# Selection of 32 keys and a gated second attention on one core: statistics under one number, half-row transposes, a minimum on VectorE, sums read block by block

## The chip, the cores and the metric

The kernel runs on one core of one Trainium2 chip. The metric is device time of one execution in microseconds, smaller is better; the time of before is the median of three runs.

## The reference

Eight batches of eight heads, 576 positions, head size 64. The first stage keeps in each row of scores the 32 largest, takes a softmax over them and multiplies by v. The second stage is an attention of four experts with a causal mask, on the first stage's output, gated to two experts a position.

```python
scores = scale * np.matmul(q, k.transpose(0, 1, 3, 2))
kth = np.partition(scores, -top_k, axis=-1)[..., -top_k:-top_k + 1]
scores = np.where(scores >= kth, scores, -1000000000.0)
attn = np.exp(scores - np.max(scores, axis=-1, keepdims=True))
attn = attn / (np.sum(attn, axis=-1, keepdims=True) + 1e-09)
x = np.matmul(attn, v)                      # heads joined: (8, 576, 512)
for e in range(4):                          # second stage
    q, k, v = x @ wq[e], x @ wk[e], x @ wv[e]
    a = softmax(scale * q @ k.T, causal)    # divided by its sum + 1e-9
    out += gate_e * (a @ v @ wo[e])         # gate: softmax over the best two of x @ w_gate
```

## The kernel before

The work is cut into 32 pairs of heads, four to a batch. A pair has nine tiles of 128 rows of scores (tile 8 holds the last 64 queries of both heads), handled three at a time.

For each three tiles TensorE computes scores (through the helper `mm`, L522), and ScalarE copies them to SBUF (L722, tile `s`). VectorE then narrows the 576 scores of a row to 168 candidates in tile `cand`. It takes the maximum of the two halves (f1, L737, into `fa`) and their minimum (f3, L740, into `fb`), the maximum of the halves of `fa` (f2, L743, into `fc`), and the maximum of the halves of `fc` (f4, L747, into `cand`). The minima that belong to f2 and f4 are computed on GpSimd, on the bit patterns as integers, as sum less maximum: L753 and L755 for f2, L760 and L762 (`lesser(2)`, `lesser(3)`) for f4. MAX8 and MATCH_REPLACE8 (L766 to L780) then find the 32 largest, eight at a time. The first replacement changes the maxima in `cand`, so it waits until L760 has read them.

The mask of what is left out is made on ScalarE (L839). TensorE transposes the scores and adds the mask times a large negative number (L915 for whole tiles, L929 and L522 for tile 8), ScalarE takes the exponential (L954, under one number `under` that holds for all rows), and TensorE multiplies by v (`av`). In tile 8 the halves of the rows belong to different heads: eight transposes of 64 rows are followed by two plain products with the identity, for the 64 keys at the ends.

The function `stats` makes each row's divisor from the 32 chosen scores: GpSimd subtracts the row's largest (L971) and writes that largest against `under` (L974), ScalarE takes the exponential (L977), VectorE the sum (L980), then follow a logarithm (L994), a subtraction on GpSimd (L998) and an exponential (L1001). L990 and L991 put a test value into the tile `ind`, which counts the candidates (L819, L826); a second, slow program runs after the first where the counts at the end don't come out.

When a batch's four pairs are done, `moe` projects q, k and v of the experts, computes scores turned round, takes exponentials into four tiles `ptm` (L1543), and makes their sums over the keys by a product with ones. Beforehand GpSimd adds the blocks of keys that meet the same queries (`plus`, L1563 to L1567, tile `prb`; VectorE in the last batch), so that this product reads the joint block once. The product with v (`avm`) reads every block.

The order is a table of task numbers, `ORDER`; each engine executes its tasks in that order. The table comes with the kernel, and dependencies and buffers set the waits.

Of the kernel before, what the change touches and what calls it, by code (L numbers as in the profile page):

```python
# [11 lines left out]
I32 = mybir.dt.int32  # L12
# [13 lines left out]
REACH = 1600.0  # L26
# [238 lines left out]
ADDED = (SUMMED[0], (512, ((0, None, 0, 0, 320), (4, 1, 448, 256, 64))))  # L265
# [240 lines left out]
def kernel(ctx, tc, qk, vL, wq, wk, wv, wo, out):  # L506
# [193 lines left out]
    def topk(w, general):  # L700
# [3 lines left out]
        for g in range(3):  # L704
# [123 lines left out]
            def later(due=pl.due, c=c, ind=w.ind, done=[t] if g < 2 else list(w.topped), compare=compare, count=count, g=g):  # L828
                keep, pl.due = pl.due, due
                a = add("POOL", 1050 if g < 2 else 1300, compare, done, bufs=[c, ind, w.top], prio=1)  # L830
                if g == 2:
                    pl.due += 0.3
                    counts.append(add("ACT", act(1530, False, 1, 1), count, [a, w.spread], bufs=[ind], prio=1))
# [935 lines left out]
```

## Time and profile before

| | us |
|---|---|
| median of three runs (lowest, highest) | 1074.46 (1070.68, 1081.57) |
| the profiled execution | 1079.49 |
| its span, first to last instruction | 1077.5 |
| TensorE busy in it | 1008.5 |
| VectorE busy | 986.6 |
| ScalarE busy | 862.2 |
| GpSimd busy | 805.6 |

Busy times are of one profiled execution. PE is TensorE, PEld its weight load, DVE VectorE, ACT ScalarE, POOL GpSimd, SP the engine that issues transfers. L747 is line 747 of the kernel before. An instruction's time runs from its start to its end and so holds what it waits for once it has begun. Idle time before an instruction is put down to what ended it. The granted clock of TensorE was 0.968 of full speed over the span.

### The profile page before, as it was taken

How to read it: one execution, taken by the hardware profiler on the slowest of the kernel's cores; microseconds unless marked ns; L12 is line 12 of the kernel's file. 1: busy time of each engine (PE TensorE's matmuls, PEld its weight loads, DVE VectorE, ACT ScalarE, POOL GpSimd, SP SyncE). 2: the span in 40 equal slices, each digit the busy share in tenths (PEclk: the TensorE clock that was granted, in tenths of full speed). 3: DMA queues.
4: the chain of work that ended last, by engine and by line, in shares of the span. 5: the costliest groups of instructions: out<-in, count | busy, mean ns of one | idle time of the engine just before them, and what ended most of it. 6: DMA issues, size and time to landing. Idle time of an engine off the chain costs nothing.

```text
span 1077.5 us, 26037 instructions
## 1 busy us (share of the span) xinstructions
PE 1008.5 (94%) x8819; PEld 730.9 (68%) x8819; DVE 986.6 (92%) x4271; ACT 862.2 (80%) x1512; POOL 805.6 (75%) x869
## 2 busy tenths in 40 slices
PE   7687889999999999999999999999999899999996
PEld 4454559666786668766886668766786657855794
DVE  8999898999999999899999999999999999999643
ACT  5676776988789896988789887899878887798744
POOL 4777776897779887898779877698769776698600
PEclk7798889999999999999999999999999999999999
DMA  3311211113113230232222131112203131120102
GB/s 114 101 42 49 73 43 55 45 42 98 51 38 90 63 91 1 70 91 86 56 70 72 43 104 51 55 50 68 84 28 84 42 103 47 43 59 13 59 2 80
DMA packets 66428, 66.21 MB, mean 61 GB/s; under 512 B 16183, under 2 KB 48878, under 8 KB 66286
## 3 DMA queue, kind: packets, MB, share of 16 engines
q1 hardware_dynamic: 66126, 64.24, 20.7%
q8 instruction: 71, 1.16, 0.4%
q14 instruction: 71, 0.58, 0.2%
q10 hardware_dynamic: 160, 0.22, 0.1%
HBM read 54.76 MB, written 9.66 MB: 60 GB/s over the span
## 4 chain that ended last, share of the span: by engine, by line
DVE 37%; PE 29%; POOL 16%; ACT 11%; issue 3%; DMA 2%; SPq 1%; POOLq 0%; DVEq 0%; ACTq 0%
PE slot L522 25%; DVE top L775 8%; DVE cand L780 8%; DVE fa L737 5%; PE slot L915 4%; DVE cand L766 4%; DVE fb L740 3%; ACT s L722 2%; DVE fc L743 2%; ACT mask L839 2%; ACT pt L954 2%; DVE cand L771 2%; DVE cand L747 2%; POOL fa L753 2%; DVE cand L770 2%
## 5 line engine op out<-in xcount | busy, mean ns | idle before, releaser
L775 DVE MAX8 top<-cand 128x8 f32<-128x72 f32 (+1 forms) x1152 | 243.4, 266 | 0.7
L839 ACT ACTIVATE mask<-s,top 128x576 bf16<-128x576 f32 x288 | 215.1, 771 | 30.8 <-DVE top L775 30.1
L954 ACT ACTIVATE pt<-slot,under 128x512 f32<-128x512 f32 (+3 forms) x320 | 217.9, 701 | 21.4 <-PE slot L522 19.0
L780 DVE MATCH_REPLACE8 cand<-top,cand 128x72 f32<-128x72 f32 (+1 forms) x864 | 206.5, 248 | 0.0
L522 PE MATMUL slot<-raw 64*128 64x288 f32 (+1 forms) x1280 | 197.3, 448 | 9.6 <-ACT s L722 5.2
L722 ACT ACTIVATE s<-slot 128x576 f32<-128x576 f32 x288 | 178.8, 649 | 32.9 <-PE slot L522 32.1
L915 PE MATMUL slot<-identr,s 128*128 128x128 f32 x1184 | 187.0, 288 | 10.1 <-ACT pt L954 4.8
L522 PE MATMUL slot<-pt,vt 128*64 128x320 f32 (+1 forms) x1280 | 174.2, 419 | 2.8 <-DMA vt<-in_vL_dram 1.8
L753 POOL TENSOR_TENSOR fa<-fa,fc 128x432 int32<-128x432 int32 x96 | 115.9, 1207 | 74.8 <-DVE fc L743 74.6
L915 PEld LDWEIGHTS slot<-identr,s 128*128 128x128 f32 x1184 | 133.5, 145 | 48.4 <-ACT s L722 10.9
L522 PE MATMUL slot<-negi,mask 128*128 128x128 bf16 (+3 forms) x1504 | 134.5, 221 | 19.0 <-ACT mask L839 18.6
L522 PEld LDWEIGHTS slot<-pt,vt 128*64 128x64 f32 x1280 | 90.4, 140 | 75.6 <-issue 7.5
L522 PEld LDWEIGHTS slot<-raw 64*128 64x128 f32 (+1 forms) x1280 | 95.7, 180 | 60.9 <-ACT s L722 12.8
L819 POOL TENSOR_TENSOR ind<-cand,top 128x504 bf16<-128x504 f32 x96 | 113.4, 1181 | 18.6 <-DVE top L775 10.4
L522 PEld LDWEIGHTS <-mask 128*128 128x128 bf16 (+2 forms) x1504 | 98.0, 100 | 42.8 <-ACT mask L839 24.3
L737 DVE TENSOR_TENSOR fa<-s 128x864 f32<-128x864 f32 x95 | 115.9, 1221 | 5.0 <-ACT s L722 3.2
L740 DVE TENSOR_TENSOR fb<-s 128x864 f32<-128x864 f32 x95 | 113.2, 1192 | 3.8 <-ACT s L722 3.2
L755 POOL TENSOR_TENSOR fa<-fa 128x432 int32<-128x432 int32 x96 | 113.5, 1182 | 3.6
L766 DVE MAX8 cand<-fb 128x8 f32<-128x288 f32 x288 | 112.1, 443 | 0.6
L760 POOL TENSOR_TENSOR cand<-fc,cand 128x216 int32<-128x216 int32 x96 | 68.7, 715 | 56.1 <-DVE cand L747 54.4
L762 POOL TENSOR_TENSOR cand<-cand,fc 128x216 int32<-128x216 int32 x96 | 72.4, 754 | 1.8
L780 DVE MATCH_VALUE_LOAD cand<-top,cand 128x8 f32 x864 | 66.8, 77 | 6.5 <-POOL cand L760 5.8
(161 smaller groups left out, 1803.4 us busy)
## 6 DMA issues: line engine op xcount, KB each, us to landing
raw<-in_qk_dram SPq DMA_DIRECT2D x127, 144.0 KB
vt<-in_vL_dram SPq DMA_DIRECT2D x32, 320.0 KB
raw<-in_qk_dram SPq DMA_DIRECT2D x127, 72.0 KB
rb<-turned SPq DMA_DIRECT2D x93, 64.0 KB
ot<-scale SPq DMA_DIRECT2D x32, 128.0 KB
out_dram<-prs SPq DMA_DIRECT2D x14, 256.0 KB
out_dram<-prb SPq DMA_DIRECT2D x14, 256.0 KB
rb<-turned SPq DMA_DIRECT2D x62, 32.0 KB
```

The costliest lines, as they stand in the source:

```text
L522: nc.tensor.matmul(o, l, r, start=start, stop=stop, skip_group_check=True)
L722: nc.scalar.activation(s3.t[:, n], sl.t[:, 224:224 + S], AF.Copy)
L737: v.tensor_tensor(out=fa.t, in0=s3.t[:, :, 0:288], in1=s3.t[:, :, 288:576], op=OP.max)
L740: v.tensor_tensor(out=fb.t, in0=s3.t[:, :, 0:288], in1=s3.t[:, :, 288:576], op=OP.min)
L753: nc.gpsimd.tensor_tensor(out=r, in0=r, in1=m, op=OP.subtract)
L755: nc.gpsimd.tensor_tensor(out=l, in0=l, in1=r, op=OP.add)
L766: v.max(out=c.t[:, n, 2, 48:56], in_=fb.t[:, n])
L775: v.max(out=w.top.t[0][:, j, 8 * r:8 * r + 8], in_=c.t[:, n, :, 0:24 if r < 2 else 55])
L780: v.match_replace(out=src, in_values=src, imm_value=LOW, in_to_replace=w.top.t[0][:, j, 8 * r:8 * r + 8])
L839: nc.scalar.activation(w.mask[j].t[:, n], s3.t[:, n], AF.Relu, bias=w.top.t[0][:, j, 31:32], scale=-1.0)
L915: nc.tensor.matmul(sl.t[:, d], src[:, c:c + P], identf, start=i % 4 == 0, stop=False, is_transpose=True, skip_group_check=True)
L954: nc.scalar.activation(out, src, AF.Exp, bias=under[r], scale=0.125)
```

## The change

Four parts, and the table `ORDER` written anew.

- Statistics: one exponential of the 32 chosen scores under the number `under`, their sum and its inverse on VectorE; GpSimd only writes the two test values (sum and inverse, each less 2.0e17) into `ind`, which grows from 1530 to 1539 elements.
- Tile 8: the two plain products become two more transposes of half rows. One of them covers 64 keys that belong to a neighbour as well, so ScalarE takes its exponential in two pieces.
- The minimum that belongs to f4 is one VectorE operation (f7) in place of L760 and L762.
- The product with ones reads every block of keys; the joint block and its additions go.

```diff
-REACH = 1600.0
+REACH = 2.0e17
...
-    IND = ring("ind", [P, 1530], BF, 1)
+    IND = ring("ind", [P, 1539], BF, 1)
...
-                if n == 2:
-                    nc.gpsimd.tensor_tensor(out=small, in0=r, in1=big, op=OP.subtract)
...
-                    nc.gpsimd.tensor_tensor(out=small, in0=small, in1=l, op=OP.add)
+            def f7(fc=fc, c=c):
+                l, r = [fc.t[:, :, o:o + 72].rearrange("p n (k a) -> p n k a", k=3) for o in (0, 72)]
+                v.tensor_tensor(out=c.t[:, :, :, 24:48], in0=l, in1=r, op=OP.min)
...
-            less = add("POOL", 600, lambda lesser=lesser: lesser(2), [t], bufs=[fc, c], prio=-8, tag="lessC")
+            t7 = add("DVE", 295, f7, [t2], bufs=[fc, c], prio=P0)
...
-            t7 = add("POOL", 600, lambda lesser=lesser: lesser(3), [less], bufs=[fc, c], prio=-8, tag="lessD")
...
-                    t = add("DVE", 3 * dve(n) + 165, lambda r=r, rep=rep: rep(r), [t] + ([less] if r == 0 else []),
+                    t = add("DVE", 3 * dve(n) + 165, lambda r=r, rep=rep: rep(r), [t],
...
-                ends = [(slice(64 * x, 64 * x + 64), o + 512 - 512 * x) for x in range(2)]
+                todo += [(lo, o + 512, slice(0, 64)), (hi, o - 64, slice(512, 576))]
...
-                for r, c in ends:
-                    mm(sl.t[r, 512:576], src[:, c:c + 64], identf[:, r])
...
-                    parts = [(al, 256, 0, 9, 64)]
+                    parts = [(al, 256, 0, 9, 64), (lo, 0, 4, 1, 64)]
...
+        def weights():
+            nc.scalar.activation(st.t[0], m32(), AF.Exp, bias=under, scale=0.125)
+
+        def inverse():
+            v.reciprocal(st.t[2], st.t[1][:, 0])
+
+        def spread():
+            g.tensor_scalar(w.ind.t[:, 1521:1530], st.t[1][:, 0], -REACH, None, op0=OP.add)
+            g.tensor_scalar(w.ind.t[:, 1530:1539], st.t[2], -REACH, None, op0=OP.add)
...
-        t = add("POOL", 760, s1, w.topped + ([] if w.general else made), bufs=b1, prio=0)
-        if not w.general:
-            t2 = add("POOL", 200, s2, w.topped + based, bufs=b1, prio=0)
-            t2 = w.spread = add("POOL", 300, spread, [t2], bufs=[st, w.ind], prio=0)
-        t = add("ACT", act(288, False), s3, [t], bufs=[st], prio=0)
-        t = add("DVE", dve(288), s4, [t], bufs=[st], prio=0)
...
+            t = add("ACT", act(288, False, 1), weights, w.topped + made + based, bufs=b1, prio=0)
+            t = add("DVE", dve(288), s4, [t], bufs=[st], prio=0)
+            t = add("DVE", 80, inverse, [t], bufs=[st], prio=0, tag="s5")
+            w.spread = add("POOL", 400, spread, [t], bufs=[st, w.ind], prio=0)
...
-                for k, n in ((0, 640), (1, 640), (2, 384)):
-                    pres.append(add("DVE" if final else "POOL", dve(n) if final else pool(n), lambda k=k, plus=plus: plus(k),
...
-                                   joint()[:, h] if u is None else ptm.t[u][r, h, o:o + m],
+                                   ptm.t[u][r, h, o:o + m],
...
-                a1 = add("PE", 1350, lambda sm=sm, weigh=weigh, joint=joint: weigh(sm, lambda r, j, h: ones[r], joint=joint),
-                         exps + pres[1:], bufs=[sm, ptm, pre], prio=3, tag="sums", kind="CC")
+                a1 = add("PE", 2750, lambda sm=sm, weigh=weigh: weigh(sm, lambda r, j, h: ones[r]), exps, bufs=[sm, ptm], prio=3,
+                         tag="sums", kind="CC")
...
 ORDER = [int(x) for x in """
-3 2 0 4 5 1 133 135 136 134 7 9 8 11 10 13 52 12 14 48 53 262 15 85 16 49 17 50 18 140 19 83 20 22 26 84 260 25 21 81
...
+3 2 0 5 1 4 128 7 9 8 11 10 13 47 12 14 51 48 248 15 49 16 6 52 17 129 83 50 18 19 81 84 127 79 20 22 82 24 244 25 23
```

On VectorE, the same three tiles in the middle of the program (the 48th of 96 groups): f2 (L743, L729 after), f4 (L747, L733 after), MAX8 `top` and MATCH_REPLACE `cand`. Before:

```order
L743 TENSOR_TENSOR fc_78<-fa_76 128x432
L747 TENSOR_TENSOR cand_80<-fc_78 128x9x24
L775 MAX top_0_84<-cand_79 128x8 x3
L766 MAX cand_80<-fb_77 128x8 x3
L775 MAX top_0_84<-cand_80 128x8 x3
L780 MATCH_REPLACE cand_80<-top_0_84,cand_80 128x3x24 x3
```

After:

```order
L729 TENSOR_TENSOR fc_78<-fa_76 128x432
L733 TENSOR_TENSOR cand_80<-fc_78 128x9x24
L748 MAX cand_80<-fb_77 128x8 x3
L757 MAX top_0_84<-cand_79 128x8 x3
L757 MAX top_0_84<-cand_80 128x8 x3
L762 MATCH_REPLACE cand_80<-top_0_84,cand_80 128x3x24 x3
L744 TENSOR_TENSOR cand_80<-fc_78 128x9x24
```

The minimum (L744) stands on VectorE, here behind the first replacement; nothing on GpSimd stands between f4 and that replacement.

On GpSimd, a pair's statistics about the middle of the program (`stat`, `ind`), between pieces of other work (`fa`, `cand` the minima, `ot` the experts' gates). Before:

```order
L753 TENSOR_TENSOR fa_76<-fa_76,fc_78 128x3x144
L755 TENSOR_TENSOR fa_76<-fa_76 128x3x144
L974 TENSOR_SCALAR stat_1_90<-top_0_84,under 128x9
L990 TENSOR_TENSOR stat_1_90<-stat_1_90 128x9
L991 TENSOR_SCALAR ind_81<-stat_1_90 128x9
L760 TENSOR_TENSOR cand_79<-fc_78,cand_79 128x9x24
L971 TENSOR_TENSOR stat_0_89<-top_0_84 128x288
L1603 TENSOR_TENSOR ot_130<-prs_122,ot_130 128x576
```

After:

```order
L959 TENSOR_SCALAR ind_81<-stat_1_90 128x9
L960 TENSOR_SCALAR ind_81<-stat_2_91 128x9
L1567 TENSOR_TENSOR ot_130<-prs_122,ot_130 128x576
L738 TENSOR_TENSOR fa_76<-fa_76,fc_78 128x3x144
L740 TENSOR_TENSOR fa_76<-fa_76 128x3x144
```

Of the statistics two small additions are left, and of the minima those of f2.

On TensorE, the sums of the last batch's first half. Before:

```order
L522 MATMUL slot_63<-ptm_0_126,ones 64x256 x2
L522 MATMUL slot_63<-ptm_1_127,ones 64x128 x2
L522 MATMUL slot_63<-prb_123,ones 64x320 x2
L522 MATMUL slot_63<-ptm_1_127,ones 64x64 x2
```

After:

```order
L509 MATMUL slot_65<-ptm_0_126,ones 64x256 x2
L509 MATMUL slot_65<-ptm_1_127,ones 64x128 x2
L509 MATMUL slot_65<-ptm_2_128,ones 64x320 x2
L509 MATMUL slot_65<-ptm_1_127,ones 64x320 x2
L509 MATMUL slot_65<-ptm_3_129,ones 64x320 x2
L509 MATMUL slot_65<-ptm_0_126,ones 64x192 x2
L509 MATMUL slot_65<-ptm_1_127,ones 64x64 x2
```

Four blocks in place of the joint one, the same seven that the product with v reads.

## Rows read from the trace of the kernel before

**Rows 1.** The page, part 1: busy us (share of the span) xinstructions.

```profile
PE 1008.5 (94%) x8819; PEld 730.9 (68%) x8819; DVE 986.6 (92%) x4271; ACT 862.2 (80%) x1512; POOL 805.6 (75%) x869
```

**Rows 2.** Three stretches: start:end length, busy PE, PEld, DVE, ACT, POOL (count), clock.

```profile
20.00:200.00 180.00, 149.83 (x1176) 105.42 (x1175) 169.70 (x763) 130.87 (x227) 130.13 (x141) 0.86 0.20 58
200.00:1013.00 813.00, 788.25 (x7095) 573.27 (x7090) 781.33 (x3396) 689.19 (x1215) 660.18 (x702) 1.00 0.22 62
1020.00:1066.00 46.00, 45.97 (x414) 37.87 (x412) 19.41 (x35) 24.83 (x46) 3.85 (x10) 1.00 0.07 20
```

**Rows 3.** The page, part 4: the chain of waits, shares of the span by engine.

```profile
DVE 37%; PE 29%; POOL 16%; ACT 11%; issue 3%; DMA 2%; SPq 1%; POOLq 0%; DVEq 0%; ACTq 0%
```

**Rows 4.** VectorE's groups (busy us, mean ns), then lines with ns min/median/max.

```profile
L737 DVE TENSOR_TENSOR fa<-s 128x864 f32<-128x864 f32 x95 | 115.9, 1221 | 5.0 <-ACT s L722 3.2
L740 DVE TENSOR_TENSOR fb<-s 128x864 f32<-128x864 f32 x95 | 113.2, 1192 | 3.8 <-ACT s L722 3.2
L743 DVE TENSOR_TENSOR fc<-fa 128x432 f32<-128x432 f32 x96 | 67.9, 707 | 4.5 <-POOL cand L762 2.5
L747 DVE TENSOR_TENSOR cand<-fc 128x216 f32<-128x216 f32 x96 | 55.6, 579 | 4.2 <-POOL ind L819 0.7
...
L737 DVE TENSOR_TENSOR fa<-s x95: 1029/1058/3219, 17.3 to 1003.0; 128x864 f32<-128x864 f32 x95
L743 DVE TENSOR_TENSOR fc<-fa x96: 580/609/1698, 9.9 to 1004.7; 128x432 f32<-128x432 f32 x96
L747 DVE TENSOR_TENSOR cand<-fc x96: 354/384/1577, 10.5 to 1007.9; 128x216 f32<-128x216 f32 x96
L1232 DVE RECIPROCAL g<-g x8: 158/174/189, 174.6 to 1048.4; 128x5 f32<-128x5 f32 x8
```

**Rows 5.** Timeline about 423 us: start us, us, engine and instruction.

```profile
423.29 1.05 DVE L740 TENSOR_TENSOR fb<-s 128x864 f32<-128x864 f32 x1
423.45 1.40 POOL L760 TENSOR_TENSOR cand<-fc,cand 128x216 int32<-128x216 int32 x1 [0.63 <-DVE cand L747]
```

**Rows 6.** GpSimd: three groups, then its busy time with tiles `stat` and `prb`.

```profile
L760 POOL TENSOR_TENSOR cand<-fc,cand 128x216 int32<-128x216 int32 x96 | 68.7, 715 | 56.1 <-DVE cand L747 54.4 <-DVE top L775 1.2
L762 POOL TENSOR_TENSOR cand<-cand,fc 128x216 int32<-128x216 int32 x96 | 72.4, 754 | 1.8
L991 POOL TENSOR_SCALAR ind<-stat 128x9 bf16<-128x9 f32 x32 | 10.9, 339 | 2.8
...
0.00:1077.50 1077.50, 83.82 (x160) 0.97 0.21 61
...
0.00:1077.50 1077.50, 65.89 (x42) 0.97 0.21 61
```

**Rows 7.** Waits: engine line <- released by: us in total, times, longest.

```profile
POOL fa L753 <- DVE fc L743: 74.6, 38, 9.5
...
DVE stat L980 <- ACT stat L977: 10.1, 8, 5.0
DVE cand L780 <- POOL cand L760: 5.8, 10, 2.0
```

**Rows 8.** ScalarE's group of exponentials of 64x128.

```profile
L954 ACT ACTIVATE pt<-slot,under 64x128 f32<-64x128 f32 x32 | 11.6, 362 | 0.6
```

**Rows 9.** TensorE's timeline, tile 8 of the last pair.

```profile
1015.51 0.46 PE L929 MATMUL slot<-identr,s 64*128 64x64 f32 x8
1015.90 0.34 PE L522 MATMUL slot<-identr,s 128*64 128x64 f32 x4
1016.17 0.44 PE L522 MATMUL slot<-negi,mask 64*128 64x64 bf16 x10
```

**Rows 10.** TensorE's timeline, sums and product with v of the last batch.

```profile
1051.61 0.87 PE L522 MATMUL slot<-ptm,ones 128*64 128x256 f32 x8
...
1053.21 3.07 PE L522 MATMUL slot<-ptm,v 128*64 128x256 f32 x28
1056.21 0.87 PE L522 MATMUL slot<-s,ones 128*64 128x256 f32 x8
```

More of the change, by code (lines that the diff above doesn't have):

```diff
@@ L749, in lesser @@
             def lesser(n, fa=fa, fc=fc, c=c):
[L750 to L762 removed]
+                l, r, m = [x.bitcast(I32) for x in (fa.t[:, :, 0:144], fa.t[:, :, 144:288], fc.t)]
+                if n == 0:
+                    nc.gpsimd.tensor_tensor(out=r, in0=r, in1=m, op=OP.subtract)
+                else:
+                    nc.gpsimd.tensor_tensor(out=l, in0=l, in1=r, op=OP.add)
+            def f7(fc=fc, c=c):
+                l, r = [fc.t[:, :, o:o + 72].rearrange("p n (k a) -> p n k a", k=3) for o in (0, 72)]
+                v.tensor_tensor(out=c.t[:, :, :, 24:48], in0=l, in1=r, op=OP.min)
             def f6(fb=fb, c=c):
@@ L832, in later @@
                     pl.due += 0.3
-                    counts.append(add("ACT", act(1530, False, 1, 1), count, [a, w.spread], bufs=[ind], prio=1))
+                    counts.append(add("ACT", act(1539, False, 1, 1), count, [a, w.spread], bufs=[ind], prio=1))
                 pl.due = keep
@@ L926, in turned @@
                         for i in range(4) for x in range(2)]
-                ends = [(slice(64 * x, 64 * x + 64), o + 512 - 512 * x) for x in range(2)]
+                todo += [(lo, o + 512, slice(0, 64)), (hi, o - 64, slice(512, 576))]
                 for i, (r, c, d) in enumerate(todo):
-                    nc.tensor.matmul(sl.t[:, d], src[r, c:c + P], identf[r, r], start=i < 2, stop=False, is_transpose=True,
+                    out, m = (sl.t[lo, d], 64) if i == 8 else (sl.t[:, d], P)
+                    nc.tensor.matmul(out, src[r, c:c + m], identf[r, r], start=i < 2, stop=False, is_transpose=True,
                                      skip_group_check=True)
-                for r, c in ends:
-                    mm(sl.t[r, 512:576], src[:, c:c + 64], identf[:, r])
-                for r, c, d in todo:
-                    mm(sl.t[:, d], mask[r, c:c + P], negi[r, r], stop=True)
-                for r, c in ends:
-                    mm(sl.t[r, 512:576], mask[:, c:c + 64], negi[:, r], stop=True)
+                for i, (r, c, d) in enumerate(todo):
+                    out, m = (sl.t[lo, d], 64) if i == 8 else (sl.t[:, d], P)
+                    mm(out, mask[r, c:c + m], negi[r, r], stop=True)
             def exp(sl=sl, pt=pt, j=j):
                 if j == 8:
-                    parts = [(al, 256, 0, 9, 64)]
+                    parts = [(al, 256, 0, 9, 64), (lo, 0, 4, 1, 64)]
                 elif j == 5:
@@ L954, in exp @@
                         nc.scalar.activation(out, src, AF.Exp, bias=under[r], scale=0.125)
-            need = [w.masked[j]] + ([w.masked[j - 1]] if j in (2, 4, 5, 7) else [w.masked[1]] if j == 0 and w.general else [])
+            need = [w.masked[j]] + ([w.masked[j - 1]] if j in (2, 4, 5, 7) else [w.masked[1]] if j == 0 and w.general else [w.masked[7]] if j == 8 else [])
             full = j in (0, 2, 4, 5, 7)
@@ L958, in turn @@
                     kind="TM" if j < 8 else "ZZ", tag="turned" if full else "turned8" if j == 8 else "turned4")
-            d = act(576, True, 1) if j == 8 else act(640, True, 1) + (200 if j == 5 else 0) if full else act(512, True, 1)
+            d = act(576, True, 1) + 200 if j == 8 else act(640, True, 1) + (200 if j == 5 else 0) if full else act(512, True, 1)
             w.es[j] = add("ACT", d, exp, [a] + ([] if w.general else based) + ([w.es[0]] if j == 5 else []), bufs=[sl, pt],
@@ L986, in s5 @@
             g.memset(z[:, 1], 0.0)
-        def spread():
-            z = st.t[1]
-            g.tensor_tensor(out=z[:, 2], in0=z[:, 1], in1=z[:, 1], op=OP.mult)
-            g.tensor_scalar(w.ind.t[:, 1521:1530], z[:, 2], -REACH, None, op0=OP.add)
         def s6():
```

47 lines of the change are left out of this document (12 added, 35 removed), and 394 rows, old and new, of the table ORDER.

## The prediction

> **What bounds the kernel now.** I read the busy times first. TensorE is busy 94% of the span, VectorE 92%, GpSimd 75% [rows 1]. An average over stages with different limits says little, so the busy time by stretch comes next [rows 2]. From 200 to 1013 us, where the selection of one pair, the product with v of another and the experts' work of a batch run beside each other, TensorE is busy 788.3 of 813 us and VectorE 781.3: 24.8 and 31.7 us idle. From 20 to 200 us the experts have no input yet; there VectorE is at 169.7 of 180 and TensorE has 30.2 us idle. After 1020 us the last batch runs on TensorE alone, 46.0 of 46 us. So in the long middle two engines are full at once, before it VectorE, behind it TensorE. The chain of waits fits: VectorE 37%, TensorE 29%, GpSimd 16% [rows 3].
>
> That GpSimd stands in the chain at all, with a quarter of its time idle, needs a reason. VectorE's operations with two inputs are much longer on average than in the median: the large maximum takes 1058 ns in the median and 1221 on average, the smallest 384 and 579 [rows 4]. Where one meets GpSimd at work, one of the two is stretched: the subtraction of L760 began 0.16 us after a VectorE minimum of 1.05 us and took 1.40 us [rows 5], against 0.715 on average [rows 6]. GpSimd's busy time of 805.6 us and the 352.6 us of these four groups make 1158 us in a span of 1077.5. They don't fit side by side; part of both is waiting for the other.
>
> **Minima on VectorE.** Gone from GpSimd are L760 (68.7 us) and L762 (72.4 us) [rows 6]. VectorE gets a minimum of the shape of L747, 96 times. At that line's median it costs 96 x 0.384 = 36.9 us; the ends are 34.0 at its shortest (0.354) and 55.6 at its mean (0.579). I take the median, because the rest of the mean is waiting, counted below. The first replacement no longer waits for L760, which gives back 5.8 us [rows 7].
>
> **Weights under one number.** GpSimd's work on the statistics, 83.8 us in all, shrinks to two small additions a pair. At L991's 339 ns these are 64 x 0.339 = 21.7 us [rows 6]. ScalarE does one exponential as before, now without waiting for GpSimd, and loses a logarithm and a small exponential. VectorE gets 32 reciprocals: at 0.174 us, a smaller one's median [rows 4], 5.6 us. VectorE's sum waits 10.1 us for that exponential today [rows 7], and the exponential waits behind GpSimd. I credit half, 5 us; nothing and 10.1 are the ends. ScalarE, at 80%, also gets a small second exponential for the last tile. That engine has room for it; without the room it would be less than 32 x 0.36 us, by the shape of 64x128 [rows 8].
>
> **Last queries in row halves.** In the last pair eight transposes start at 1015.51 and the four records of the two plain products at 1015.90, the mask products at 1016.17 [rows 9]. So eight transposes cost 0.39 us and the plain products 0.27. Two more transposes at 0.05 each replace them: 0.17 us a pair, 5.4 in all. Nothing to 0.27 x 32 = 8.6 are the ends. The mask products stay ten.
>
> **Sums over every block.** GpSimd loses 65.9 us of additions [rows 6]. TensorE's product with ones gets the shape of the product with v beside it. In the tail the one starts at 1051.61, the other at 1053.21, the next sum at 1056.21 [rows 10]: 1.60 against 3.00 us, so +1.40, and 16 times +22.4 us. All of it lies on the fullest engine. The two of the last batch (+2.8 us) lie behind the last selection, where nothing else can take the time. The additions that VectorE did there leave, but VectorE waits in that stretch, busy 19.4 of 46 us [rows 2]; I cost them at nothing.
>
> **The sum.** TensorE gets 22.4 - 5.4 = +17.0 us. On VectorE the waiting on GpSimd is (mean - median) x count of the four groups: 15.5 + 12.7 + 9.4 + 18.7 = 56.3 us [rows 4], with L737's median for its twin L740 too. GpSimd loses 68.7 + 72.4 + 83.8 + 65.9 - 21.7 = 269 of 805.6 us, a third. I take a third off the waiting, -18.8 us, and give the new minimum two thirds of its twin's 0.195 us, +12.5. VectorE's balance is 36.9 + 5.6 - 18.8 + 12.5 - 5.8 - 5.0 = +25.4 us. Its ends are -38 (shortest minimum, all 56.3 us of waiting and both waits gone, the reciprocals hidden) and +55 (the twin's mean, no relief but the 5.8).
>
> What of this reaches the end? If TensorE sets the pace and idles as now, +17.0; if half of its 24.8 us of idle time in the middle is filled, +4.6. If VectorE sets it, +25.4 and the tail's 2.6, so +28; with half of its 31.7 us of idle time filled, +12. Both must hold, and the two ranges meet from +12 to +17. I take **+14 us**. The profiled execution took 1079.5 us (span 1077.5 and 2.0 around it), which gives 1093.5; it lies 5.0 over the median of the runs, 1074.5. From the median the forecast is **1088.5 us**, 1.3% slower.
>
> The order is written anew on all engines, but keeps its shape: the same 640 score products on TensorE, the experts of each batch behind the same pairs, the last batch's whole behind the last scores. I see no stage that moves, and cost the reordering at nothing; it is why my ranges are wide.
>
> **Rivals.**
> *The meeting of GpSimd and VectorE was the bound (faster).* For it: 1158 us of work in 1077.5, GpSimd's 16% (172 us) of the chain, and GpSimd's long wait for VectorE, 74.6 us at L753 [rows 3, 7]. Against it: an engine that is 74.6 us early in one place isn't what the others wait for there, and TensorE is nearly full in the same stretch. After the change GpSimd has 536 us and the two-input work about 383, 919 in place of 1158. If that freed the loop, TensorE would be next: 17.0 more work less all 24.8 us of idle time is -8, and some 4 us out of the 30.2 idle before 200 us make -12, so 1062 us.
> The Trainium skill, page "SBUF — State Buffer", section "SBUF: two separate sides", says that VectorE's operations with two inputs in SBUF and GpSimd's share a pair of ports under an exclusive lock, and that whoever comes second blocks for the whole instruction. The trace agrees [rows 5]: 1.40 us for a short subtraction. By that rule alone the moved minima would pay (141.1 us of holding the pair become 36.9), and this rival would be the forecast. I don't make it so, because the row of the middle stretch has TensorE, which doesn't use that pair, at 97%.
>
> *The relief pays for the additions (same).* The waiting on VectorE falls by half rather than a third and most of the statistics' wait goes: 36.9 + 5.6 - 28 + 9 - 5.8 - 10 = +8, with the idle time of both engines a little better filled: 1068 to 1083 us, about 1076.
>
> *VectorE pays in full (slower, beyond the forecast).* The new minimum meets GpSimd as often as its twin, at 0.579 us, and nothing else is relieved: 55.6 + 5.6 - 5.8 = +55 at the worst; with the third off the old waiting, +36.6 and 2.6 in the tail: 1114 us. It decides once the two-input operations' mean stays above their median as now.
>
> *The change doesn't do what it says.* The check at the end now tests the sums and their inverses against 2.0e17. If it failed, the slow second program would run after the first and the time would be a multiple. The limits follow the new count (1539 for 1530), so I give it 1%. Milder: half-row transposes that cost what the products cost leave +22.4 on TensorE, 1094 us.
>
> **How the numbers follow.** Forecast (1086 to 1097 us) 0.36; VectorE in full (above) 0.20; relief pays 0.28; the meeting was the bound 0.15; the check 0.01. A measurement of this kernel tells about 1% from no change, so 1064 and 1085 are the limits. Slower: 0.33 of the forecast, 0.20 and 0.01, 0.54. Same: 0.28, 0.03 of the forecast and 0.02 of the faster rival, 0.33. Faster: 0.13. The range goes from 1064, TensorE's floor with a little to spare, to 1108, +28 with the minimum halfway to its worst; the forecast's own range is 1086 to 1097.
>
> **What would show it.** Right: TensorE's busy time about 1025 us, its sums 3.0 us; VectorE's about 1020, the new minimum at 0.38 in the median; GpSimd near 540; idle time of TensorE from 200 us to the last selection about as now; the last selection ends near 1025 rather than 1013. Wrong: if the means of the two-input operations drop to their medians and TensorE's idle time in the middle halves, the relief was worth more than I gave it; if VectorE's idle time grows, a wait that I did not see took the place of those removed.

## The result and the profile after

The kernel after takes **1059.92 us** in the median of 4 runs (1057.71 to 1061.11), before 1078.01 (4 runs beside it, 1070.68 to 1081.77). The ratio is 0.9835, 95% interval [0.9802, 0.9868]: 1.65% faster. I had said 1088.5 us, slower, in a range from 1064 to 1108, and gave faster by over 1% a chance of 0.13. The forecast was wrong, and the time lies below the range too. The profiled execution took 1061.11 us (span 1059.1), the one of before 1079.49.

The page of after, busy times and the chain of waits by engine, against [rows 1, 3]:

```profile
PE 1000.3 (94%) x8947; PEld 738.0 (70%) x8947; DVE 980.1 (93%) x4393; ACT 860.5 (81%) x1480; POOL 524.7 (50%) x539
...
PE 52%; DVE 30%; ACT 8%; POOL 3%; SPq 3%; issue 2%; DMA 2%; DVEq 0%; POOLq 0%; ACTq 0%
```

GpSimd has lost 281 us of work and left the chain (16% before, 3% now). VectorE got 122 instructions more and is busy 6.5 us less. TensorE got 128 more and is busy 8.2 us less.

VectorE's groups of after, busy us and mean ns, against [rows 4] (L723 was L737, L726 L740, L729 L743, L733 L747; L744 and L956 are new):

```profile
L723 DVE TENSOR_TENSOR fa<-s 128x864 f32<-128x864 f32 x95 | 104.4, 1099 | 5.1 <-ACT s L708 3.3
L726 DVE TENSOR_TENSOR fb<-s 128x864 f32<-128x864 f32 x95 | 102.9, 1083 | 0.2
L729 DVE TENSOR_TENSOR fc<-fa 128x432 f32<-128x432 f32 x96 | 60.6, 632 | 1.4
L733 DVE TENSOR_TENSOR cand<-fc 128x216 f32<-128x216 f32 x96 | 44.3, 461 | 4.2 <-POOL ind L800 0.9
L744 DVE TENSOR_TENSOR cand<-fc 128x216 f32<-128x216 f32 x96 | 43.7, 456 | 1.0
...
L956 DVE RECIPROCAL stat<-stat 128x9 f32<-128x9 f32 x32 | 6.6, 207 | 0.9
```

The four old groups were 352.6 us and are 312.2, by 40.4 us shorter. The new minimum costs 43.7, so all five take what four took before.

Who waits now, against [rows 7]:

```profile
POOL fa L738 <- DVE fc L729: 243.1, 75, 10.9
...
DVE stat L966 <- ACT stat L953: 7.6, 4, 5.8
```

GpSimd stands ready for f2's result in 75 of 96 groups (38 before) and waits 243.1 us for it (74.6). The first replacement's wait for GpSimd (5.8 us) is gone, that of the sum for ScalarE is 7.6 in place of 10.1.

The same stretches as in [rows 2]. The kernel ends 19 us earlier now, so the third stretch holds other work than before and its row says little:

```profile
20.00:200.00 180.00, 149.15 (x1200) 104.91 (x1201) 176.43 (x806) 134.45 (x229) 90.52 (x91) 0.89 0.18 52
200.00:1013.00 813.00, 801.42 (x7361) 595.93 (x7358) 776.60 (x3499) 696.27 (x1203) 424.59 (x431) 1.00 0.22 63
1020.00:1066.00 46.00, 30.65 (x288) 22.79 (x286) 10.87 (x24) 19.70 (x34) 3.67 (x10) 0.93 0.16 50
```

The cut that explains most is another one: from the start to the end of the last MAX8 of the selection. It ends at 1013.4 us before and at 994.6 after. What follows takes 64 us in both (1077.5 - 1013.4 and 1059.1 - 994.6). So the whole gain lies ahead of that point, and VectorE's row there tells its kind (before, then after; VectorE's busy time is the third after the length):

```profile
0.00:1013.40 1013.40, 953.69 (x8330) 686.74 (x8331) 966.57 (x4234) 829.24 (x1454) 796.66 (x852) 0.97 0.22 63
```

```profile
0.00:994.60 994.60, 944.24 (x8438) 692.63 (x8439) 964.23 (x4361) 828.41 (x1424) 517.09 (x525) 0.98 0.22 64
```

VectorE: 2.3 us less work, 16.5 us less idle time (46.8 to 30.4). Together they are the 18.8 us. Of the idle time, waits for GpSimd went from 17.4 to 8.8 us and waits for ScalarE from 31.0 to 23.4, when the rows of VectorE's waits over the whole span are added up by releaser.

### The profile page after: what moved, and what is told of

Its sections match the earlier page's. It is cut to its first block, busy times and chain, and to the rows that moved or that the text cites. A ratio compares the mean times of both kernels' runs of the same rounds, so it can differ in the third digit from the quotient of the medians.

```text
span 1059.1 us, 25954 instructions
## 1 busy us (share of the span) xinstructions
PE 1000.3 (94%) x8947; PEld 738.0 (70%) x8947; DVE 980.1 (93%) x4393; ACT 860.5 (81%) x1480; POOL 524.7 (50%) x539
## 4 chain that ended last, share of the span: by engine, by line
PE 52%; DVE 30%; ACT 8%; POOL 3%; SPq 3%; issue 2%; DMA 2%; DVEq 0%; POOLq 0%; ACTq 0%
PE slot L509 44%; PE slot L896 7%; DVE top L757 6%; DVE cand L762 6%; DVE fa L723 3%; DVE cand L748 3%; DVE fb L726 3%; ACT mask L820 2%; ACT s L708 2%; DVE fc L729 2%; ACT pt L933 2%; SPq L1034 2%; DVE cand L744 1%; DVE cand L752 1%; DVE cand L753 1%
## 5 line engine op out<-in xcount | busy, mean ns | idle before, releaser
L757 DVE MAX8 top<-cand 128x8 f32<-128x165 f32 (+1 forms) x1152 | 243.3, 267 | 1.0
L933 ACT ACTIVATE pt<-slot,under 128x640 f32<-128x640 f32 (+4 forms) x352 | 226.8, 667 | 21.1 <-PE slot L509 17.8
L738 POOL TENSOR_TENSOR fa<-fa,fc 128x432 int32<-128x432 int32 x96 | 117.2, 1220 | 245.8 <-DVE fc L729 243.1
L762 DVE MATCH_REPLACE8 cand<-top,cand 128x72 f32<-128x72 f32 (+1 forms) x864 | 206.9, 249 | 0.0
L509 PE MATMUL slot<-raw 64*128 64x288 f32 (+1 forms) x1280 | 190.9, 442 | 14.0 <-DMA raw<-in_qk_dram 6.7
L509 PE MATMUL slot<-pt,vt 128*64 128x320 f32 (+1 forms) x1280 | 170.1, 414 | 4.2 <-DMA vt<-in_vL_dram 3.1
L896 PEld LDWEIGHTS slot<-identr,s 128*128 128x128 f32 x1184 | 131.4, 144 | 40.9 <-ACT s L708 10.9
L509 PE MATMUL slot<-negi,mask 128*128 128x128 bf16 (+2 forms) x1504 | 137.0, 218 | 16.3 <-ACT mask L820 16.0
L509 PEld LDWEIGHTS <-mask 128*128 128x128 bf16 (+2 forms) x1504 | 102.4, 100 | 37.5 <-ACT mask L820 21.8
L740 POOL TENSOR_TENSOR fa<-fa 128x432 int32<-128x432 int32 x96 | 110.4, 1150 | 5.6
L723 DVE TENSOR_TENSOR fa<-s 128x864 f32<-128x864 f32 x95 | 104.4, 1099 | 5.1 <-ACT s L708 3.3
L726 DVE TENSOR_TENSOR fb<-s 128x864 f32<-128x864 f32 x95 | 102.9, 1083 | 0.2
L1065 POOL TENSOR_TENSOR av<-av,rb 128x576 f32<-128x576 f32 x31 | 46.8, 1511 | 42.3 <-DMA rb<-turned 31.6
L762 DVE MATCH_VALUE_LOAD cand<-top,cand 128x8 f32 x864 | 67.3, 78 | 0.0
L752 DVE MAX8 cand<-fa 128x8 f32<-128x72 f32 x288 | 63.0, 219 | 4.1 <-POOL fa L740 2.0
```

The lines of the kernel that those rows point to most:

```text
L509: nc.tensor.matmul(o, l, r, start=start, stop=stop, skip_group_check=True)
L723: v.tensor_tensor(out=fa.t, in0=s3.t[:, :, 0:288], in1=s3.t[:, :, 288:576], op=OP.max)
L726: v.tensor_tensor(out=fb.t, in0=s3.t[:, :, 0:288], in1=s3.t[:, :, 288:576], op=OP.min)
L738: nc.gpsimd.tensor_tensor(out=r, in0=r, in1=m, op=OP.subtract)
L740: nc.gpsimd.tensor_tensor(out=l, in0=l, in1=r, op=OP.add)
L757: v.max(out=w.top.t[0][:, j, 8 * r:8 * r + 8], in_=c.t[:, n, :, 0:24 if r < 2 else 55])
```

## The experiments

The question after the result: the sum had VectorE's balance, waits included, at +25.4 us, and it came out at -18.8. Three theories. **Meeting**: lighter GpSimd work by itself frees VectorE's two-input operations. **Order**: the new table is what pays. **My sum**: the parts cost what I said, and something else gained.

Names that begin with b_ have the order of before, those with a_ that of after, but for the three with "plan". The table holds all twenty kernels, each cut at the end of its last selection: VectorE's busy time until then, what is left of the stretch (idle), and two columns counted from the rows of the trace. "Behind" is the number of f1, f3, f2, f4 and f7 that began while a two-input GpSimd instruction was already under way. "Excess" is their time above the mean of the others of their line, in us.

| run | selection ends | VectorE busy | idle | behind | excess |
|---|---|---|---|---|---|
| before | 1013.4 | 966.6 | 46.8 | 200 of 382 | 59.8 |
| after | 994.6 | 964.2 | 30.4 | 103 of 478 | 27.7 |
| b_all | 1049.2 | 1013.3 | 35.9 | 169 of 478 | 77.8 |
| b_minima | 1053.2 | 1027.2 | 26.0 | 222 of 478 | 96.7 |
| b_sums | 1018.3 | 959.9 | 58.4 | 179 of 382 | 53.3 |
| b_stats | 1008.2 | 971.4 | 36.8 | 168 of 382 | 60.9 |
| b_halves | 1014.8 | 965.8 | 49.0 | 198 of 382 | 59.2 |
| b_minima_near | 1084.6 | 1059.9 | 24.7 | 234 of 478 | 131.0 |
| b_drop | 1021.1 | 981.1 | 40.0 | 175 of 382 | 75.6 |
| a_none | 1177.5 | 964.6 | 212.9 | 139 of 382 | 49.7 |
| a_no_sums | 1061.5 | 990.3 | 71.2 | 135 of 478 | 52.1 |
| a_junk | 1038.3 | 1010.5 | 27.8 | 234 of 478 | 74.7 |
| a_memset | 1024.3 | 991.5 | 32.8 | 124 of 478 | 55.2 |
| b_all_f4 | 1049.4 | 1009.9 | 39.5 | 150 of 478 | 71.6 |
| b_all_f43 | 1045.7 | 992.3 | 53.4 | 127 of 478 | 55.0 |
| a_f4_late | 1000.1 | 975.0 | 25.1 | 123 of 478 | 40.2 |
| a_f4_near | 1002.1 | 972.0 | 30.1 | 100 of 478 | 35.6 |
| a_plan | 1099.7 | 1073.8 | 25.9 | 210 of 478 | 136.2 |
| a_plan_free | 1119.3 | 1066.5 | 52.8 | 300 of 478 | 133.4 |
| b_plan | 1111.4 | 967.2 | 144.2 | 165 of 382 | 60.1 |

### The parts in the order of before

Each part, and all four together, with the table of before carried over: every task keeps its place, a new one takes the place of the one it replaces (f7 that of L762).

```diff
+ f7 on VectorE, without lesser(2) and lesser(3)      (b_minima, b_all)
+ ptm block by block for the product with ones        (b_sums, b_all)
+ weights, inverse, spread                            (b_stats, b_all)
+ todo += [(lo, o + 512, ...), (hi, o - 64, ...)]     (b_halves, b_all)
  ORDER: the sequence of before
```

> All four parts of the change, but in the order of the kernel before (the statistics' new instructions take the places of the old ones, the new minimum takes the place of L762). If the parts themselves pay, because GpSimd and VectorE meet less, the time is near the changed kernel's, 1060 to 1066 us, and the waiting of VectorE's two-input operations (mean less median, times count) is near 18 us for the four old groups, as there. If the new order is what pays, the time is near before's or above it, 1075 to 1095 us, though GpSimd's busy time falls to about 525 us here too. My sum, which was wrong for the changed kernel, would give 1090 us.

> Before with one part: the minimum that belongs to f4 on VectorE, in the place of L762; L760 and L762 gone from GpSimd (141 us). If meeting is what bounds, the waiting of the four old two-input groups falls from 56 us to 35 or less, and the time is 0 to 1% lower in spite of 37 us more on VectorE. By my sum VectorE gets 30 us more and the time is 1085 to 1095 us.

> Before with one part: the product with ones reads every block; 66 us gone from GpSimd, 22.4 us more on TensorE. If TensorE sets the pace the time rises by 15 to 22 us, to 1090 or more. If GpSimd's part of the chain (18 us on L1563 to L1567) was what was waited for there, the time is within 0.5% of before.

> Before with one part: the statistics under one number; GpSimd loses 62 us, VectorE gets 32 reciprocals (5.6 us). If meeting is what bounds, the time falls by 0.5 to 1.5% (5 to 16 us), since nothing is added that counts; by my sum it falls by 5 us or less.

> Only the halves part (two half-row transposes and two copies into pt in place of the two plain products), in the order of before. My sum: 5.4 us less on TensorE, between 0 and 8.6; where VectorE sets the pace nothing of it reaches the end in the middle: 1070 to 1079. If the parts add up in the old order (b_all +40.2; minima +41.1, sums +12.6, statistics -5.1), the halves alone are worth about -8: 1067 to 1072.

Measured: all four **1118.26 us**, ratio 1.0370 [1.0346, 1.0394]. The minima alone 1119.06, 1.0389 [1.0370, 1.0407]; the sums alone 1090.09, 1.0119 [1.0100, 1.0138]; the statistics alone 1072.67, 0.9953 [0.9936, 0.9970]; the halves alone 1080.26, 1.0022 [1.0010, 1.0034]. So the same work as in after costs 40.6 us in the old order, with the places that I gave the new instructions there, and gains 18.1 in the new one: the table is worth 58 us. The parts alone add up to +41.4 + 12.5 - 5.0 + 2.0 = +50.9, 10 more than all four together. Against the expectations, all four and the minima lie above every range that I had named, and the waiting of the four old groups stayed at 55.4 and 62.7 us (56.3 before) where the meeting theory wanted 18 and 35 or less; the sums just reach the 1090 us of one side, with a rise of 12.5 us for the 15 to 22 named; the statistics lie on the border of both sides; the halves lie a little above mine.

The halves show what a saving on TensorE is worth here. It is busy 1002.2 us in place of 1008.5, 6.3 less where the sum had 5.4, and nothing reaches the end.

VectorE's groups in b_all, the lines of f3, f4 and f7, and the stretch to the end of the selection:

```profile
L728 DVE TENSOR_TENSOR fb<-s 128x864 f32<-128x864 f32 x95 | 122.6, 1291 | 1.5 <-ACT s L710 0.9
...
L735 DVE TENSOR_TENSOR cand<-fc 128x216 f32<-128x216 f32 x96 | 64.0, 667 | 4.2 <-DVE fc L731 0.5
...
L746 DVE TENSOR_TENSOR cand<-fc 128x216 f32<-128x216 f32 x96 | 51.0, 531 | 0.0
```

```profile
0.00:1049.20 1049.20, 971.24 (x8444) 697.28 (x8444) 1013.27 (x4361) 830.47 (x1425) 540.48 (x526) 0.97 0.21 61
```

GpSimd is as light here as in after (546.8 us busy against 524.7), and yet f3 takes 1291 ns on average (after 1083), f4 667 (461), f7 531 (456). VectorE is busy 49.1 us longer to the end of the selection, and the excess is 50.1 us larger. A lighter GpSimd alone does not keep the two apart. What it does give in the old order is idle time: VectorE's falls from 46.8 us to 35.9 in b_all, and its waits for GpSimd over the whole span from 17.4 us to 9.4. Of the 16.5 us less idle time in after, 10.9 are there before the order changes.

### GpSimd's load taken away, with nothing in its place

```diff
-less = add("POOL", 600, lambda lesser=lesser: lesser(2), ...
-t7 = add("POOL", 600, lambda lesser=lesser: lesser(3), ...
+nc.vector.memset(tile_, LOW)                 (once, at the start)
```

> The kernel before with both subtractions and additions of the third minima left out (96 L760 and 96 L762 on GpSimd), no minimum on VectorE in their place; the places for them hold a constant filled in once, and the closing test never asks for the second program, so a part of the selection is left out. Every engine keeps its order of before. Meeting theory (lighter GpSimd pays by itself): VectorE's two-input waiting falls from 56 us to below 30, and the time to 1055 us or less. Order theory: the waiting stays above 40 us and the time between 1062 and 1078. My sum: 5.8 us and about half of 18.8 off, so 1062 to 1066.

Measured: **1085.98 us**, 1.0071 [1.0050, 1.0093]. GpSimd is busy 657.9 us in place of 805.6 and the kernel is slower. Each theory had it at 1078 or less. The excess grew from 59.8 to 75.6 us: GpSimd is late less often (it stands ready for f2's result in 62 groups, 38 before) and starts its subtraction of f2's minima right behind f2, and 61 f4 begin behind a GpSimd operation (46 before). This is what felled the meeting theory as I had put it.

### One instruction moved

```diff
 f4
+f7
 ...
-f7          (was at the place of L762)
```

> Only the minima part, in the order of before; the new minimum stands directly behind the minimum of L743's group (f4) and no longer in the place of the second subtraction's end. Order theory (the 96 minima cost much because every engine's order was laid out for the old durations): one instruction's place changes little, 1105 to 1120 us, two-input waiting still above 60 us. Rival, the place of that one instruction made the 41 us: 1090 us or less, waiting near 50. My sum for this part alone (36.9 - 5.8 + part of 12.5, less some relief): about 1100.

Measured: **1150.24 us**, 1.0647 [1.0613, 1.0681], 31 us slower than with the minimum further off. Neither side of the expectation held, and the rows say why. VectorE and GpSimd about 422 us in this run, two rows of each:

```profile
422.70 0.38 DVE L744 TENSOR_TENSOR cand<-fc 128x216 f32<-128x216 f32 x1
423.09 1.20 DVE L755 TENSOR_TENSOR cand<-fc 128x216 f32<-128x216 f32 x1
```

```profile
422.74 1.31 POOL L749 TENSOR_TENSOR fa<-fa,fc 128x432 int32<-128x432 int32 x1 [3.20 <-DVE fc L740]
424.13 1.14 POOL L751 TENSOR_TENSOR fa<-fa 128x432 int32<-128x432 int32 x1
```

f4 begins 0.04 us ahead of GpSimd's subtraction and takes its short 0.38 us. f7 begins behind it and lasts 1.20 us, to 0.24 us past the end of GpSimd's operation. So do most: 76 of 96 f7 begin behind GpSimd, and the mean of all is 1057 ns, 101.5 us in sum. In the kernel after the same meeting looks like this, about 430 us:

```profile
429.86 0.61 DVE L729 TENSOR_TENSOR fc<-fa 128x432 f32<-128x432 f32 x1
430.57 0.38 DVE L733 TENSOR_TENSOR cand<-fc 128x216 f32<-128x216 f32 x1
430.61 1.31 POOL L738 TENSOR_TENSOR fa<-fa,fc 128x432 int32<-128x432 int32 x1 [3.23 <-DVE fc L729]
430.99 0.51 DVE L757 MAX8 top<-cand 128x8 f32<-128x72 f32 x3
432.00 1.12 POOL L740 TENSOR_TENSOR fa<-fa 128x432 int32<-128x432 int32 x1
432.01 0.50 DVE L757 MAX8 top<-cand 128x8 f32<-128x72 f32 x3
433.02 0.38 DVE L744 TENSOR_TENSOR cand<-fc 128x216 f32<-128x216 f32 x1
```

Beside GpSimd's two operations (430.61 to 433.12) stands work with one input, and f7 comes when they are nearly over. Work with one input is not slowed: MAX8 over 165 columns takes 0.316 us on average inside a two-input GpSimd operation (250 of them in after) and as much clear of any (221).

So a fourth theory: **who begins first**. A two-input operation of VectorE that begins ahead of GpSimd's costs its short time; one that begins behind waits for the rest of it. In after, f1 takes 1.047 us on average where no two-input operation of GpSimd's lies beside it, 1.052 where it begins first (8 cases), 1.423 where it begins second; f4 0.370, 0.380 and 0.690. GpSimd's subtraction of f2's minima, in its turn, takes 1.11 us alone or first and 1.34 where it begins inside one of VectorE's (47 of 96).

### GpSimd's load added to the kernel after

```diff
+add("POOL", 600, junk, [t2], prio=P0)        (twice a group, behind f7's add)
+    nc.gpsimd.tensor_tensor(out=JUNK, in0=JUNK, in1=JUNK, op=OP.subtract)     (a_junk)
+    nc.gpsimd.memset(JUNK.bitcast(FT), 0.0)  (three times)                    (a_memset)
```

> The kernel after, with two more GpSimd subtractions of 128x216 int32 a group on a tile of their own that nobody reads (192 in all, some 0.7 us each, about 135 us of GpSimd's time). All other engines' order as in after. Meeting theory: VectorE's two-input waiting rises from 25 us to above 45 and the time by 20 us or more, to 1080. Order theory: GpSimd has half its time free, waiting rises by 10 to 20 us, and the time stays below 1070.

> The kernel after with six GpSimd fills of a private 128x216 tile a group, at the places where the run with two added subtractions had these (that run: 1106.8 us, two-input waiting 68.9 us); a fill reads nothing. Meeting theory (two-input operations of VectorE wait for GpSimd only where both read): the waiting stays below 35 us and the time below 1070 us, though GpSimd is loaded by about as much. If GpSimd's load as such costs (its own work comes later, whatever it is): 1090 us or more.

Measured: subtractions 1106.78 us, 1.0256 [1.0218, 1.0294], on the side of the meeting theory (1080 or more); fills 1091.33 us, 1.0126 [1.0103, 1.0149]. The load is 150.1 and 160.1 us:

```profile
L793 POOL TENSOR_TENSOR junk<-junk 128x216 int32<-128x216 int32 x192 | 150.1, 782 | 8.0 <-DVE junk L620 0.4
```

```profile
L794 POOL MEMSET junk<- 128x216 f32 x576 | 160.1, 278 | 28.1 <-DVE junk L620 0.4
```

Operations of VectorE that begin inside one of these and meet nothing else of GpSimd's: inside a subtraction 101, with means of 1.192 (f1), 1.214 (f3), 0.765 (f2), 0.593 (f4) and 0.560 (f7); inside a fill 106, with 1.046, 1.042, 0.601, 0.371 and 0.366, their short times. A fill, which reads nothing, does not hold VectorE up. The Trainium skill says as much on its page "SBUF — State Buffer", section "SBUF: two separate sides": an operation of VectorE with two inputs in SBUF shares the pair of ports with GpSimd only against a GpSimd operation that reads, and whoever starts first has it for the whole instruction. The trace agrees.

But the fills cost 31 us all the same, where I had said less than 10. The time is that of the other side of the expectation (1090 us or more), though not by its reason, that GpSimd's own work comes later: some of it comes earlier. With a fill ahead of it in its queue, GpSimd's subtraction of f2's minima begins 0.08 us behind f2's end in the median and not 0.14, and f4 stands at 0.10. GpSimd and then VectorE at two places of that run:

```profile
440.19 1.11 POOL L750 TENSOR_TENSOR fa<-fa,fc 128x432 int32<-128x432 int32 x1 [0.84 <-DVE fc L741]
...
568.27 1.31 POOL L750 TENSOR_TENSOR fa<-fa,fc 128x432 int32<-128x432 int32 x1
```

```profile
440.22 1.33 DVE L745 TENSOR_TENSOR cand<-fc 128x216 f32<-128x216 f32 x1
...
568.23 0.39 DVE L745 TENSOR_TENSOR cand<-fc 128x216 f32<-128x216 f32 x1
```

Thirty ns behind GpSimd: 1.33 us. Forty ns ahead: 0.39. The f4 directly behind f2 have a mean of 0.842 us here (41) and of 0.505 in after (40). VectorE is busy 27.3 us longer to the end of the selection, and the excess is 27.5 us larger: the added load did its harm through who came first.

### Single operations moved on VectorE

```diff
 f2
+f4              (b_all_f4, b_all_f43: 37 groups; a_f4_near: 30 groups)
 MAX8 or MATCH_REPLACE
-f4
...
+f3              (b_all_f43 as well: 37 times)
 f2
-f3
...
 f2
-f4              (a_f4_late: 27 groups)
 one task of MAX8 or MATCH_REPLACE
+f4
```

> The four parts in the order of before (the kernel that took 1118.3 us), and VectorE's order alone changed: in 37 groups the maximum of 24 (f4), which stood one to three operations behind the maximum of 144 (f2), is moved directly behind it. GpSimd starts its subtraction 0.14 us after f2; of the 39 f4 that began 0.15 to 2.6 us after f2 the mean was 0.854 us, of those directly behind 0.504. Meeting theory (who begins first at the shared port decides): 37 x 0.35 = 13 us off VectorE, time 1104 to 1110 us. Rival (the gain of the new order lies in the filling of TensorE or in the queue of GpSimd, and a stretched operation only moves elsewhere): within 4 us of 1118.

> As the run with f4 moved, and in 37 groups the minimum of 288 (f3) is moved ahead of an f2 that stood less than 2.5 us before it, so that it no longer begins inside GpSimd's two operations behind f2 (27 such f3 had a mean of 1.492 us, the others 1.211). Meeting theory: another 37 x 0.28 = up to 10 us off VectorE, 1094 to 1104 us. Rival: f2 and with it GpSimd and the selection come 1 us later in 37 groups, nothing is won, 1104 or more; or all within 4 us of 1118 if meetings only move.

> The kernel after, VectorE's order alone changed: in 27 of the 40 groups where f4 stands directly behind f2 it is moved behind the next task of one-input operations, so that it begins inside GpSimd's subtraction. Meeting theory: 27 x 0.35 = 9.5 us more on VectorE, and time 1066 to 1074 us. Rival (the place of f4 doesn't matter, after's gain comes from elsewhere): 1058 to 1063.

> The kernel after, VectorE's order alone changed: 30 f4 that stood a few operations behind f2 are moved directly behind it, where VectorE begins 0.04 us ahead of GpSimd. Who-begins-first theory: the 26 f4 that began behind a GpSimd operation become about 15, 11 x 0.3 = 3 us less on VectorE, time 1054 to 1060. Rival, the one-input work that stood between now lies elsewhere and moves others into GpSimd's way: 1060 to 1068.

Measured: b_all_f4 1116.82 us, 1.0358 [1.0341, 1.0375]; b_all_f43 1114.98, 1.0349 [1.0333, 1.0365]; a_f4_late 1070.22, 0.9933 [0.9918, 0.9948]; a_f4_near 1068.49, 0.9904 [0.9890, 0.9918].

In the old order the time is that of the rival in both expectations, within 4 us of 1118. The moved operations themselves did what was expected of them: f4 begun behind GpSimd went from 51 to 21, f3 with the second move from 46 to 33. But with f4 moved alone, f3 went from 46 to 55 behind. With both, VectorE has 21 us less work and 17.5 us more idle time, so only 3 us reach the end. Seven of the 17.5 are waits for the sum of f2's minima, which now comes later (8.5 us in place of 1.5); where the others come from is open.

In the new order f4 moved late costs 10.3 us, as expected; moved near, where I had hoped for 3 us less, 8.6. There f4 behind GpSimd did fall from 26 to 14, but the work that had stood between shifted, f7's mean rose from 456 to 515 ns, and each f4 that was still behind took 1.029 us in place of 0.690. The rival that I had named held. The new table lies in a narrow place: both shifts of one operation cost nearly 1%. No version beats after.

### Old work in the new order, and a third order

```diff
  ORDER: the sequence of after
+ all four parts of before (a_none); the additions of before (a_no_sums)
...
-for t in pl.listed(ORDER):
+for t in pl.order():          (a_plan, a_plan_free, b_plan)
+    PORT = ()                 (a_plan_free)
```

> The four parts of before in the order of after: new order, old work (the subtraction behind f4, the addition at the place of the new minimum, the old statistics and the additions before the product with ones). If the new order is simply better for any work: 1060 us or less. If it pays because it fits the new work's durations: slower than before, 1085 to 1120 us, two-input waiting above 56 us and GpSimd's queue late. If the order is worth nothing (my sum): 1070 to 1080.

> The kernel after with the sums part undone: additions on GpSimd (and six on VectorE) before the product with ones, which reads the halves as before; the additions stand where their inputs are ready. My sum: TensorE gets 22 us back, GpSimd 62 us of additions more: if TensorE sets the pace 1040 to 1048. If the new order keeps VectorE clear of a GpSimd at half load, and the additions bring meetings back: 1060 to 1075. In the order of before this part alone cost 12.5 us.

> The work of after, its order not from the table but laid out by the list scheduler in the kernel's own code (class Plan), whose rule that a two-input operation doesn't begin while GpSimd works also counts the new minimum. The order is another on every engine. If the change itself is a gain under equal layout: faster than the same scheduler's order for the work of before. Expected 1080 to 1130 us; two-input waiting 25 to 45 us.

> As the run before it, but the scheduler is told nothing of the meeting of GpSimd and VectorE. If minding it is what an order gains by: two-input waiting 55 to 80 us and the time 15 to 40 us above the run that minds it. If not: within 10 us of it.

> The work of before, its order laid out by the same scheduler with its rule on the meeting. My sum (the change costs 14 us whatever the order): 10 to 20 us faster than the scheduler's order for the work of after. If the change pays once each work has an order of its own: 15 us or more slower than it, as 1078 stands to 1060.

Measured: old work in the new order **1244.94 us**, 1.1523 [1.1482, 1.1563], far beyond the 1120 that I had as the upper end. VectorE has as much to do as in after (964.6 us) and stands idle 213, and GpSimd's subtraction behind f4 blocks its queue:

```profile
POOL cand L761 <- DVE cand L748: 138.3, 76, 10.0
```

The new order is no better in itself; it fits the new work. With only the additions put back it takes 1127.18 us, 1.0453 [1.0435, 1.0470], 67 us above after and outside both sides of the expectation, while the sums alone cost 12.5 us in the old order. Where the additions stand there was my choice, so this bounds nothing; it shows how little the table bears.

Laid out by one and the same scheduler, the new work takes 1160.11 us, 1.0765 [1.0743, 1.0788], the old 1173.92, 1.0888 [1.0864, 1.0913]: the change is 14 us faster, just under the 15 that I had set for the case that it pays, although the scheduler put every f7 directly behind its f4, where they cost 1226 ns on average:

```profile
L744 DVE TENSOR_TENSOR cand<-fc 128x216 f32<-128x216 f32 x96 | 117.7, 1226 | 0.0
```

Without its rule on the meeting it makes 1187.94, 1.1027 [1.1004, 1.1050]. The 28 us are not VectorE's stretched operations (133.4 us of excess against 136.2) but its idle time (52.8 against 25.9), with 6 us more behind the selection, and GpSimd is busy 657.5 us in place of 567.5. So the time differs as I had expected, but not by the meeting: the rule did not lower the excess, which is above before's 59.8 in both runs, and the time with the rule lies above the 1130 that I had as its upper end.

## Why the prediction was wrong

The step that failed is "I see no stage that moves, and cost the reordering at nothing". In the old order the four parts cost 40.6 us; the new table takes 58 of them back. I looked for moved stages and found none. What moved were single VectorE operations against GpSimd's, within a microsecond.

The second failed step hangs on it: waiting in proportion to GpSimd's load ("I take a third off the waiting, -18.8 us"). Load is not what decides. At the same light load the four old groups wait (mean less median, as in the prediction) 55.4 us in the old order, 17.5 in the new one, against 56.3 before. So relief is 0.9 or 38.8 us, by the order alone. The new minimum's own waiting was 7.7 us where I had put 12.5, in the old order 15.2.

The other terms, as the prediction named them:

- *Minima at the median, 36.9 us.* The median is 0.376 us, as taken. But an operation on VectorE begins about 0.08 us before the record of the one ahead ends: f7 at 433.02 with 0.38 us is followed by MAX8 at 433.31. From start to start it is 0.293 us in the median, so the stream got 28.1 us longer and not 36.9. The reciprocals are 0.207 us in the record and 0.127 from start to start: 4.1 us, not 5.6. With the change of the excess, 28.1 + 4.1 - 32.1 = +0.1; the cut had -2.3.
- *The tail, +2.6.* Next to nothing: 64.1 us before, 64.5 after.
- *Both waits.* The replacement's 5.8 us went. Of the statistics' 10.1 us 2.5 went, where I had credited 5; the part alone was worth 5.0 us in time.
- *Sums, +1.40 each.* The shape was right:

```profile
1031.26 3.07 PE L509 MATMUL slot<-ptm,ones 128*64 128x256 f32 x28
1034.26 3.07 PE L509 MATMUL slot<-ptm,v 128*64 128x256 f32 x28
```

  3.00 us from start to start. Alone, the part added 14.6 us to TensorE's busy time, where I had 22.4, and 12.5 to the time; 5.1 us came behind the last selection, where I had 2.8.
- *Halves, -5.4 on TensorE.* It was -6.3, and at the end nothing.
- *TensorE about 1025 us.* It came to 1000.3. The two parts alone sum to +8.3, so some 16 us went elsewhere. With the same matmuls in the old order it is busy 1028.3 us (b_all), so the term held there and the order takes 28 off. Part of that may be the clock: it was granted at 0.979 over the span against 0.969 in b_all, and at 0.89 against 0.87 from 20 to 200 us. From 200 us to the end of the selection it is 1.00 in both, and a matmul still takes 108.9 ns of busy time in place of 111.7 (783.0 us for 7192, 814.3 for 7288), so about 20 us are not the clock, an estimate from these two stretches. What they are is open.
- *VectorE about 1020, selection ending near 1025 us.* 980.1 and 994.6. GpSimd near 540: 524.7, right.
- *What would show it wrong*: the means fell towards the medians, as that sentence said; TensorE's idle time in the middle went from 24.8 to 11.6 us.

The rival "the meeting of GpSimd and VectorE was the bound" gave 1062 us and came nearest the time. Its mechanism was only half right. It held that less load would free the loop; with less load and the old order the loop got slower. What the rows show is the lock and its order. The Trainium skill's rule on that page, which I had cited, says who blocks: the one that comes second. I turned it into microseconds of GpSimd's load, and that is not what it says. Against the rival I held TensorE at 97% in the middle; but it filled to 98.6%, and the time followed VectorE: what follows the selection takes 59 to 69 us in all twenty kernels of the table, VectorE is idle in only 3% of the stretch ahead of it in after, and where a change added work to VectorE in the new order (a_f4_late, a_f4_near, a_memset, a_junk: +10.8, +7.8, +27.3, +46.3) the end of the selection went with it (+5.5, +7.5, +29.7, +43.7).

"VectorE pays in full" came near for the old order: 1114 us by its working, and all four parts took 1118 there. Part of that is luck: it had the new minimum at 0.579 us and a third off the old waiting, and there the minimum took 0.531 and the waiting lost 0.9 us in place of 18.8.

Shown: who begins first sets an operation's length; in after fewer begin second (103, and 169 in b_all), and with the same work VectorE is busy 49 us less for it, of the 57.5 by which the two spans differ. Not shown: why VectorE's idle time falls, by 10.9 us with the parts in the old order and by 5.5 more in the new one; what part TensorE's 28 us less busy time has in it; and how the table came to be. Nor is work taken off VectorE always time: b_all_f43 took 21 us off it and ended 3 us sooner than b_all.

## What to carry to other kernels

Where two engines can hold each other up, price a moved operation by what stands beside it in the new order: look which of the two begins first, and count, rather than scale a sum of waiting by load. A part tried in the old order can lose 40 us and with an order of its own gain 18, so neither number alone is the part's worth. Then look whether the work saved became idle time on the same engine. And take an added instruction's cost from start to start in the timeline, not from its record.

## What the runs showed of the hardware

- A minimum of 128x216 takes 0.38 us beginning 0.04 us ahead of a GpSimd subtraction of 128x432 and 1.33 us beginning 0.03 us behind it. One that begins first is hardly slowed (f1 1.052 against 1.047 us alone, 8 cases).
- A GpSimd fill of 128x216 (0.278 us) does not slow VectorE's two-input operations (106 of them at their short times); a subtraction of the same shape (0.782 us) does (101 of them; f1 takes 1.192 us there and 1.046 inside a fill).
- Taking 148 us of busy time off GpSimd made the kernel 0.7% slower: 61 f4 began behind a GpSimd operation in place of 46, and the excess rose from 59.8 to 75.6 us.
- Successive VectorE records overlap by about 0.08 us (median in before and after), so an added minimum of 0.376 us takes 0.293 from start to start.
